# Attention backward: reciprocals of the softmax row sums moved from VectorE to GpSimd, and the row factors spread over four iterations

## The chip, the cores and the metric

One NeuronCore of a Trainium2 chip runs one program. The metric is the device time of the program in microseconds; the figure before the change is the median of three runs, 2174.07 us (2173.19 to 2174.79). A profile is one further execution, taken with the hardware profiler. The engines are named as in the profile: PE (TensorE's matmuls), PEld (its weight loads), DVE (VectorE), ACT (ScalarE), POOL (GpSimd) and SP (SyncE, which here only issues DMAs).

## The reference

What is computed is the output and all gradients of

```python
xn = layernorm(x)
s = attention(xn, wqkv, wo)           # 32 heads of 16, 2048 rows, softmax(q k^T / 4) v
g = silu(mlp(xn, w1, b1, w2, b2))     # layernorm, 512 -> 1792 (gelu) -> 512
out = x + s * g
```

with x of 2048 x 512 in bf16, for a given gradient of `out`. The change touches the attention alone. Per row of queries it needs L (the sum of the exponentials, the softmax' denominator), 1/L, and delta = (row sum of p times dp) in the form of a sum that is divided by L. With them O, dQ, dK and dV are formed.

## The kernel before

The program has three stages: projections, MLP forward and all preparations (to about 220 us), the attention forward and backward in one pass (to about 1845 us), and the remaining gradients.

**The attention's loop.** `attention_core` goes over 64 blocks: 16 pairs of heads (`p`) times 4 chunks of 512 queries (`qc`). A block has 16 iterations, one per 128 keys, so the loop variable `g` runs over 1024 iterations and 20 more, and g % 16 is the iteration within a block. The order of all instructions is written out by hand in the loop body (L1395 to L1445); each engine executes its own instructions in that order. In iteration g:

- `emit_d(g)` and `emit_s(g + 1)` (PE): dp^T of this iteration, in two halves into three rotating PSUM buffers (`d`), and the scores of the next one into a single PSUM buffer (`s`).
- `emit_exp(g + 1)` (ACT, L1155): the exponentials `ets`.
- `emit_z(g - 20)` (PE, L1365): the sums `Z` for dK and dV of a block that began 20 iterations earlier. Their weights are W2 (first four of eight iterations, one query chunk of 128 in each: iterations 4 to 7 and 12 to 15 of a block) and W1 (the other four: iterations 8 to 11, and 0 to 3). Iteration 4 thus reads the part of W2 for the first query chunk of the block before, iteration 6 the one for the third.
- `emit_x(g - 1)` (PE, L1263, L1266, L1270): the sums `X` for O, L, delta and dQ; the last group reads `gts`, DVE's product of the iteration before.
- `emit_T(g - 1)` (PE, L1223, L1227): transposes of the exponentials into one PSUM buffer `tT`, which `emit_cT` (ACT, L1239) and `emit_cO` (DVE, L1246) copy to `ek`.
- `emit_mult(g)`: POOL copies a part of `ets` to `gts` (L1184), DVE forms the two products `gts` = d times ets (L1186). Between the two products stand, where due, the copy of X (L1279, in iteration 0) and `emit_acc` (DVE, L1377, L1379): the sum of Z over the query chunks, in iterations 3 and 11. After the last query chunk of a pair of heads `emit_acc` also lets POOL cast the sum (`ob`, L1383) and issue two DMAs that store it (L1386). For one half of the sums that falls into iteration 11 of a pair's first block, for the other into iteration 3 of its second block.
- `emit_dmat(g)` (SP): a DMA transpose of every second `gts` to `gk`, which Z reads later. `gts` has four buffers, each for two iterations.
- Loads of the next pair's operands are issued from POOL's queue in chosen iterations (6, 9, 12, 15), each behind a tiny copy (`tick`, L1435) that waits for DVE's product of that iteration.

**The end of a block.** When a block's X is complete, DVE copies it (`xs`), PE transposes it in two halves (`emit_XT`, iterations 1 and 6 of the next block), and at the start of the iteration after (2 and 7) DVE copies the transposed half back (`emit_xt`, L1305) and `emit_fin` runs. For the half that holds L (iteration 2): DVE's reciprocal rL (L1325), then POOL's chain: W2 = q times rL (L1326), ndl = delta sum times rL (L1328), ndr = ndl times rL (L1330), and the two halves of W1 (L1331, L1332). For the other half (iteration 7): O, and dQ over four instructions (L1337 to L1344). W2 has one buffer, W1 two. For the last block both halves run in the iterations right after the loop's last block, with no attention beside them.

Of the kernel before, what the change touches and what calls it, by code (L numbers as in the profile page):

```python
# [9 lines left out]
f32 = mybir.dt.float32  # L10
ACT = mybir.ActivationFunctionType
ALU = mybir.AluOpType
# [1069 lines left out]
def attention_core(ctx, ctx_r, tc, k, grads, Oall, dQall, dKVT_out, ident_f32, ident_bf, npairs=16, nqc=4):  # L1082
    nc = tc.nc
# [13 lines left out]
    finp = sb("finp", 1)  # L1097
# [13 lines left out]
    W2 = wp.tile([128, 4, 2, 32], bf16, name="W2")  # L1111
    nc.gpsimd.memset(W2[:, :, :, 0:16], 0.0)
    for i in range(2):
        W1 = wp.tile([128, 4, 2, 32], bf16, name=f"W1_{i}")
# [6 lines left out]
    blk = [dict(Gk={}, Ek={}) for _ in range(NB)]  # L1121
    cur = {}

    def a_unit(g):
        return (g // 16, g % 16) if 0 <= g < NSTEP else None
# [178 lines left out]
        j, h = f  # L1304
        nc.vector.tensor_copy(out=blk[j]["xs"][:, 256 * h:256 * h + 256], in_=blk[j].pop("XT"))  # L1305

    def emit_fin(g):
        f = fin_half(g)
        if f is None:
            return  # L1310
        j, half = f
        p, qc = blocks[j]
        NQq = k.op0["NATQq"]
        NQd = k.op0["NATQd"]
        xf = blk[j]["xs"][:]
        XE = xf[:, 0:256].rearrange("q (b h c) -> q b h c", b=4, h=2)
        XG = xf[:, 256:512].rearrange("q (b h c) -> q b h c", b=4, h=2)
        W1, W2 = WT[j % 2]
        st0 = qc * 4
        nqs = NQq[:, st0:st0 + 4, :, :]  # L1320
        ndo = NQd[:, st0:st0 + 4, :, :]
        bc = lambda ap: ap.to_broadcast([128, 4, 2, 16])
        if half == 1:
            rL = finp.tile([128, 4, 2, 1], f32, name="rL")
            nc.vector.reciprocal(out=rL[:], in_=XG[:, :, :, 17:18])  # L1325
            nc.gpsimd.tensor_tensor(out=W2[:, :, :, 16:32], in0=nqs, in1=bc(rL[:]), op=ALU.mult)  # L1326
            ndl = finp.tile([128, 4, 2, 1], f32, name="ndl")
            nc.gpsimd.tensor_tensor(out=ndl[:], in0=XG[:, :, :, 0:1], in1=rL[:], op=ALU.mult)  # L1328
            ndr = finp.tile([128, 4, 2, 1], f32, name="ndr")
            nc.gpsimd.tensor_tensor(out=ndr[:], in0=ndl[:], in1=rL[:], op=ALU.mult)  # L1330
            nc.gpsimd.tensor_tensor(out=W1[:, :, :, 0:16], in0=ndo, in1=bc(rL[:]), op=ALU.mult)  # L1331
            nc.gpsimd.tensor_tensor(out=W1[:, :, :, 16:32], in0=nqs, in1=bc(ndr[:]), op=ALU.mult)  # L1332
            blk[j]["r"] = rL, ndl
            return
        rL, ndl = blk[j].pop("r")
        Ov = Oall[:, st0:st0 + 4, p * 32:(p + 1) * 32].rearrange("q b (h c) -> q b h c", h=2)
        nc.gpsimd.tensor_tensor(out=Ov, in0=XE[:, :, :, 16:32], in1=bc(rL[:]), op=ALU.mult)  # L1337
        t1 = finp.tile([128, 4, 2, 16], f32, name="t1")
        nc.gpsimd.tensor_tensor(out=t1[:], in0=XE[:, :, :, 0:16], in1=bc(ndl[:]), op=ALU.mult)
        nc.gpsimd.tensor_tensor(out=t1[:], in0=XG[:, :, :, 1:17], in1=t1[:], op=ALU.add)  # L1340
        rL4 = finp.tile([128, 4, 2, 1], f32, name="rL4")
        nc.gpsimd.tensor_scalar(out=rL4[:], in0=rL[:], scalar1=0.25, scalar2=None, op0=ALU.mult)
        dQv = dQall[:, st0:st0 + 4, p * 32:(p + 1) * 32].rearrange("q b (h c) -> q b h c", h=2)
        nc.gpsimd.tensor_tensor(out=dQv, in0=t1[:], in1=bc(rL4[:]), op=ALU.mult)  # L1344
        blk[j].pop("xs")
# [49 lines left out]
    for g in range(NSTEP - ZOFF):  # L1395
        cur["g"] = g
        a = a_unit(g)
        if a is not None:
            j, kb = a
            p, qc = blocks[j]  # L1400
            if kb == 0 and qc == 0:
                L = natq_loads(k, k.op0, p, nc.gpsimd.dma_start) if p > 0 else []
                if p + 1 < npairs:
                    L += op_load_list(k, OP[(p + 1) % 2], p + 1, nc.gpsimd.dma_start)
                else:
                    L += grads.tail_loads(nc.gpsimd.dma_start)
                for i, f in enumerate(L):
                    late.append((g + 16 * (i // 4) + 6 + 3 * (i % 4), f))
        emit_cO(g - 2)
        if a_unit(g - 2) is not None:  # L1410
            emit_xt(g - 1)
            emit_fin(g - 1)
        emit_d(g, 0)
        emit_s(g + 1, 0)
        emit_s(g + 1, 1)
        emit_d(g, 1)
        emit_exp(g + 1)
        emit_z(g + ZOFF)
        emit_x(g - 1, "e")
        emit_x(g - 1, "l")  # L1420
        if g % 16 == 2:
            emit_x(g - 2, "g")
        if g % 16 != 1:
            emit_x(g - 1, "g")
        st_T.pop(g - 2, None)
        emit_T(g - 1)
        emit_XT(g)
        emit_mult(g)
        if a_unit(g - 1) is None:
            emit_xt(g)  # L1430
            emit_fin(g)
        for it in [x for x in late if x[0] <= g]:
            late.remove(it)

            nc.gpsimd.tensor_copy(out=tick[:], in_=st_gt[g][0:1, kb % 2, 7, 126:128])  # L1435
            it[1]()
        if g >= NSTEP:
            grads.tail_mid(g - NSTEP)
        emit_cT(g - 1)
        emit_dmat(g)  # L1440
        st_gt.pop(g - 3, None)
        st_et.pop(g - 12, None)
        if g == NSTEP:
            ctx_r.close()
            grads.tail_open(ps_t, ps_s, ps_d)  # L1445


def full_kernel(ctx, tc, A_x, A_wqkv, A_wo, B_x, B_w1, B_b1, B_w2, B_b2, grad_out,
                out_0, out_1, out_2, out_3, out_4, out_5, out_6, out_7, dbg=None):
    nc = tc.nc  # L1450
    dbg = dbg or {}
    k = K()
    persist = ctx.enter_context(tc.tile_pool(name="persist", bufs=1))
    k.ident_bf = persist.tile([128, 128], bf16, name="ident_bf")
    make_identity(nc, k.ident_bf[:])
    k.ident_f = persist.tile([128, 128], f32, name="ident_f")
    make_identity(nc, k.ident_f[:])
    k.eps_t = persist.tile([128, 1], f32, name="eps_t")
    nc.vector.memset(k.eps_t[:], EPS)
    k.rstd1 = persist.tile([128, NT], f32, name="rstd1")  # L1460
    k.rstd2 = persist.tile([128, NT], f32, name="rstd2")
    persist.tile([128, 224], mybir.dt.uint8, name="pad_to_256")

    def scratch(name, shape, dt=bf16):
        if name in dbg:
            return dbg[name]
        return tc.dram_tile(list(shape), dt, name=name)
    k.XN_s = scratch("XN_s", [S, D])
    k.Y_s = scratch("Y_s", [S, D])
    k.DSO_s = scratch("DSO_s", [S, D])  # L1470
    k.H1T_s = scratch("H1T_s", [F, S])
    k.HGT_s = scratch("HGT_s", [F, S])
    k.WKV_s = scratch("WKV_s", [D, 1024])
    k.DH1_s = scratch("DH1_s", [4, 4, 128, 4, 4, 128])
    k.NAT_s = scratch("NAT_s", [NPAIR, 128, NT, 2 * NATW])
    k.NATQq_s = scratch("NATQq_s", [NPAIR, 128, NT, 32])
    for n in ("KT_s", "VT_s", "QT_s", "DOT_s"):
        setattr(k, n, scratch(n, [D, S]))
    k.UT_s = scratch("UT_s", [H, S])
    k.NATQd_s = scratch("NATQd_s", [NPAIR, 128, NT, 32])  # L1480
    k.GB_s = scratch("GB_s", [S, 2, D])
    k.dKVT_s = scratch("dKVT_s", [H * 32, S])

    with ExitStack() as cO, tc.manual_schedule():
        op0p = cO.enter_context(tc.tile_pool(name="op0", bufs=1, side="right", reuse_waits="tile"))
        k.op0 = make_op(nc, op0p, 0)
        k.Lc = op0p.tile([128, 32], bf16, name="Lc")
        nc.gpsimd.memset(k.Lc[:], 0.0)
        nc.gpsimd.memset(k.Lc[:, 17:18], 1.0)
        op0p.tile([128, 96], mybir.dt.uint8, name="pad_to_256r")  # L1490
        kv, nat, q, do, natd = op_loads(k, k.op0, 0, nc.sync.dma_start)
        first = dict(kv=kv, q=lambda: (nat(), q()), do=lambda g: (do(g * 512, g * 512 + 512), natd(g * 4, g * 4 + 4)))
        with ExitStack() as cP:
            Pre(cP, tc, k, first, A_x, A_wqkv, A_wo, B_w1, B_b1, B_w2, B_b2, grad_out)
        pO = cO.enter_context(tc.tile_pool(name="persistO", bufs=1, reuse_waits="tile"))
        k.Oall = pO.tile([128, NT, D], bf16, name="Oall", tag="Oall")
        k.dQall = pO.tile([128, NT, D], bf16, name="dQall", tag="dQall")
        grads = Grads(cO, tc, k, pO, op0p, A_x, grad_out, A_wqkv, A_wo, B_w1, B_w2,
                      (out_0, out_1, out_2, out_3, out_4, out_5, out_6, out_7))
        with ExitStack() as cB:  # L1500
            attention_core(cB, cB.enter_context(ExitStack()), tc, k, grads, k.Oall, k.dQall, k.dKVT_s, k.ident_f, k.ident_bf)
        grads.run()
# [56 lines left out]
```

## Time and profile before

| what | value |
|---|---|
| median of three runs | 2174.07 us |
| the profiled execution | 2176.54 us, of which the span of the trace is 2174.8 us |
| attention, first to last exponential's start | 210 to 1832 us of the span |
| PE, DVE, ACT, POOL busy in 640 to 840 us | 200.0, 187.0, 184.5, 83.8 us of 200 |
| DVE reciprocal (L1325) | 64 x 203 ns |
| POOL's chain for W2 and W1 (L1326 to L1332) | 398, 197, 204, 402, 401 ns each |

The first part of the profile's page gives busy time per engine, the groups of instructions give line, engine, operation, the tiles written and read, the count, the busy time in us with the mean in ns, and the idle time of the engine before them with what ended it. The timeline gives start, duration, line, operation and count of neighbouring instructions of one kind. The waits list who waited for whom: total us, number of times, the longest. Matmuls overlap in PE, and one that waits in PE's queue counts as busy.

### The profile page before, as it was taken

What the parts mean: (1) busy time and instruction counts of PE and PEld (TensorE: products, weight loads), DVE (VectorE), ACT (ScalarE), POOL (GpSimd) and SP (SyncE); (2) the same over time, 40 slices, a digit from 0 to 9 for tenths busy, and PEclk for the clock granted to TensorE, in tenths of its full rate; (3) what the DMA queues carried; (4) which work ended last, traced back from release to release, by engine and by line L of the source; (5) the groups of instructions that cost most, each with busy time, mean ns of one, the idle gap of its engine ahead of it and who ended that gap; (6) DMA issues with size and microseconds to landing.
All of it is one profiled execution on the core that took longest, in us unless ns stands there. A gap on an engine that the chain in (4) does not pass through costs nothing.

```text
span 2174.8 us, 74927 instructions
## 1 busy us (share of the span) xinstructions
PE 2135.9 (98%) x30663; PEld 1169.9 (54%) x30663; DVE 1900.2 (87%) x3524; ACT 1781.4 (82%) x2482; POOL 868.4 (40%) x2396
## 2 busy tenths in 40 slices
PE   7998999999999999999999999999999999999999
PEld 4444555555555555555555555555555555444444
DVE  7677899999999999999999999999999998897637
ACT  5754999999999999999999999999999997784214
POOL 4286334343444434343444344444434344510003
PEclk9999999999999999999999999999999999999999
DMA  7986999999999999999999999999999999999875
GB/s 243 275 275 211 187 203 199 203 205 201 202 206 199 204 201 200 206 199 194 206 201 204 201 207 201 198 207 200 200 207 204 197 213 222 283 267 233 235 207 176
DMA packets 1416601, 461.17 MB, mean 212 GB/s; under 512 B 1329150, under 2 KB 1400446, under 8 KB 1416256
## 3 DMA queue, kind: packets, MB, share of 16 engines
q1 hardware_dynamic: 1401952, 425.44, 101.3%
q0 software_dynamic: 12720, 29.37, 4.8%
q8 instruction: 240, 3.93, 0.8%
q10 hardware_dynamic: 1584, 1.57, 0.2%
q14 instruction: 105, 0.86, 0.1%
HBM read 62.79 MB, written 64.75 MB: 59 GB/s over the span
## 4 chain that ended last, share of the span: by engine, by line
PE 93%; DMA 3%; DVE 3%; ACT 1%; POOL 1%; issue 1%; SPq 0%; DVEq 0%; POOLq 0%; ACTq 0%
PE tT L1223 22%; PE d L1168 15%; PE Z L1365 15%; PE X L1270 6%; PE X L1263 5%; PE X L1266 5%; PE s L1146 3%; PE ps_dy L940 2%; PE ps_h L374 2%; PE ps_m L389 2%; PE ps_dw L1014 2%; PE ps_dw L773 2%; PE ps_dh L906 2%; PE ps_dwkv L858 1%; PE tT L1297 1%; PE ps_dxa L1058 1%
## 5 line engine op out<-in xcount | busy, mean ns | idle before, releaser
L1186 DVE TENSOR_TENSOR gts<-d,ets 128x512 bf16<-128x512 f32 x2048 | 1302.5, 683 | 20.0 <-PE d L1168 4.4
L1155 ACT ACTIVATE ets<-s 128x1024 bf16<-128x1024 f32 x1024 | 1051.3, 1027 | 16.2 <-PE d L1168 3.6
L1239 ACT COPY ek<-tT 128x448 f32<-128x448 f32 (+1 forms) x1024 | 524.7, 512 | 118.0 <-PE tT L1223 29.6
L1223 PE MATMUL tT<-ident_bf,ets 128*128 128x128 bf16 x6790 | 557.9, 221 | 0.0
L1223 PEld LDWEIGHTS <-ets 128*128 128x128 bf16 x6790 | 382.4, 98 | 211.0 <-issue 196.7
L1168 PE MATMUL d<-QDT,KVT 32*128 32x512 bf16 x2048 | 470.3, 384 | 2.7 <-DVE gts L1186 2.6
L1184 POOL COPY gts<-ets 128x128 bf16<-128x128 bf16 x1024 | 280.2, 295 | 391.2 <-ACT ets L1155 383.6
L1146 PE MATMUL s<-QDT,KVT 32*128 32x512 bf16 x2048 | 400.9, 379 | 3.0 <-ACT ets L1155 2.4
L1365 PE MATMUL Z<-gk,W 128*32 128x512 bf16 x2304 | 302.9, 389 | 1.3 <-DVE acc L1379 1.1
L1263 PE MATMUL X<-ets,NAT 128*32 128x256 bf16 x4096 | 290.4, 273 | 0.0
L1266 PE MATMUL X<-ets,Lc 128*32 128x256 bf16 x4096 | 290.2, 273 | 0.0
L1270 PE MATMUL X<-gts,NAT 128*17 128x256 bf16 x4096 | 289.8, 273 | 0.0
L1365 PEld LDWEIGHTS <-W 128*32 128x32 bf16 x4096 | 105.5, 93 | 240.0 <-issue 226.2
L1168 PEld LDWEIGHTS <-KVT 32*128 32x128 bf16 x2048 | 148.3, 90 | 114.4 <-issue 21.5
L1365 PE MATMUL Z<-ek,W 128*32 128x512 bf16 x1792 | 203.7, 389 | 0.0
L1266 PEld LDWEIGHTS <-Lc 128*32 128x32 bf16 x4096 | 110.2, 97 | 108.5
L1246 DVE COPY ek<-tT 128x64 f32<-128x64 f32 x378 | 85.0, 225 | 88.1 <-ACT ek L1239 72.5
L1435 POOL COPY tick<-gts 1x2 bf16<-1x2 bf16 x205 | 35.7, 174 | 313.9 <-DVE gts L1186 313.9
L1146 PEld LDWEIGHTS <-KVT 32*128 32x128 bf16 x2048 | 142.6, 90 | 13.4 <-issue 7.2
L1270 PEld LDWEIGHTS <-NAT 128*17 128x17 bf16 x4096 | 114.0, 91 | 14.5 <-issue 1.7
L1263 PEld LDWEIGHTS <-NAT 128*32 128x32 bf16 x4096 | 108.8, 96 | 7.2 <-issue 7.2
L1326 POOL TENSOR_TENSOR W<-NATQq,rL 128x128 bf16<-128x128 bf16 x64 | 25.4, 398 | 148.0 <-DVE rL L1325 115.7
(256 smaller groups left out, 2476.2 us busy)
## 6 DMA issues: line engine op xcount, KB each, us to landing
gk<-gts SPq DMA_TRANSPOSE x512, 5.4
H1T_s<-h1r SPq DMA_DIRECT2D x28, 256.0 KB, 3.2
HGT_s<-hgT SPq DMA_DIRECT2D x8, 896.0 KB, 4.6
DH_s<-stg SPq DMA_DIRECT2D x12, 512.0 KB, 3.6
hch<-DH_s SPq DMA_DIRECT2D x12, 512.0 KB, 4.8
gp<-H1T_s SPq DMA_DIRECT2D x9, 512.0 KB, 5.4
out_dram<-ob_w POOLq DMA_DIRECT2D x36, 128.0 KB, 4.1
NAT_s<-NS SPq DMA_DIRECT2D x4, 1056.0 KB, 5.9
```

The source lines that it names most:

```text
L1146: nc.tensor.matmul(s[:, hj, :], lhsT=op["KVT"][r:r + 32, kb * 128:(kb + 1) * 128], rhs=op["QDT"][r:r + 32, qc * 512:(qc + 1) * 512], start ...
L1155: nc.scalar.activation(out=st_et[g].rearrange("k b h q -> k h b q"), in_=cur["s"][:].rearrange("k h (b q) -> k h b q", b=4), func=ACT.Exp)
L1168: nc.tensor.matmul(d[:], lhsT=op["KVT"][r:r + 32, kb * 128:(kb + 1) * 128], rhs=op["QDT"][r:r + 32, qc * 512:(qc + 1) * 512], start=True, ...
L1184: nc.gpsimd.tensor_copy(out=gts[:, kb % 2, 8, :], in_=st_et[g][:, b // 2, b % 2, :])
L1186: nc.vector.tensor_tensor(out=gts[:, kb % 2, 4 * hj:4 * hj + 4, :], in0=st_d.pop((g, hj))[:].rearrange("k (b q) -> k b q", b=4), in1=st_et ...
L1223: nc.tensor.transpose(tb[:, i - cut(g), :], et[:, b // 2, b % 2, :], ident_bf[:])
L1239: nc.scalar.copy(out=blk[j]["Ek"][kb // 4][:, kb % 4, c:7].rearrange("q i k -> q (i k)").bitcast(f32), in_=st_T[g][:, 0:(7 - c) * 64])
L1246: nc.vector.tensor_copy(out=blk[g // 16]["Ek"][kk // 4][:, kk % 4, i].bitcast(f32), in_=st_T[g][:, 448:512])
L1263: nc.tensor.matmul(X[r:r + 32, 0:256], lhsT=NATt[:, kb, hj, 1:33], rhs=ev, start=(kb == 0), stop=False, skip_group_check=True, tile_positi ...
L1266: nc.tensor.matmul(X[r:r + 32, 256:512], lhsT=Lc[:], rhs=ev, start=False, stop=False, skip_group_check=True, tile_position=(0, r))
L1270: nc.tensor.matmul(X[r:r + 17, 256:512], lhsT=NATt[:, kb, hj, 0:17], rhs=gv, start=False, stop=(kb == 15), skip_group_check=True, tile_pos ...
L1365: nc.tensor.matmul(Z[r:r + 32, :], lhsT=WT[j % 2][1 - part][:, qb, hj, :], rhs=mv, start=(part == 0 and qb == 0), stop=(part == 1 and qb = ...
```

## The change

The reciprocal leaves DVE. POOL forms it as L to the power -1 and one Newton step, r (2 - L r), for the first two query chunks of 128 with the first half of W2 in iteration 2, and for the other two in iteration 3. The rest of the chain follows in iteration 4 (ndl, ndr, first half of W1) and iteration 5 (second half of W1). Of the second half, O is formed in iteration 7 and dQ in iteration 8. All these pieces now stand after `emit_mult` of their iteration and no longer at its start. For the last block the four pieces run one after the other in one iteration. A constant tile of -1 (32 bytes per partition) is added and the padding is cut by as much.

```diff
-    def emit_fin(g):
+    def emit_fin(g, ph):
         f = fin_half(g)
-        if f is None:
+        if f is None or (f[1] == 0 and ph > 1):
             return
...
         if half == 1:
-            rL = finp.tile([128, 4, 2, 1], f32, name="rL")
-            nc.vector.reciprocal(out=rL[:], in_=XG[:, :, :, 17:18])
-            nc.gpsimd.tensor_tensor(out=W2[:, :, :, 16:32], in0=nqs, in1=bc(rL[:]), op=ALU.mult)
-            ndl = finp.tile([128, 4, 2, 1], f32, name="ndl")
-            nc.gpsimd.tensor_tensor(out=ndl[:], in0=XG[:, :, :, 0:1], in1=rL[:], op=ALU.mult)
-            ndr = finp.tile([128, 4, 2, 1], f32, name="ndr")
-            nc.gpsimd.tensor_tensor(out=ndr[:], in0=ndl[:], in1=rL[:], op=ALU.mult)
-            nc.gpsimd.tensor_tensor(out=W1[:, :, :, 0:16], in0=ndo, in1=bc(rL[:]), op=ALU.mult)
-            nc.gpsimd.tensor_tensor(out=W1[:, :, :, 16:32], in0=nqs, in1=bc(ndr[:]), op=ALU.mult)
-            blk[j]["r"] = rL, ndl
-            return
-        rL, ndl = blk[j].pop("r")
+            if ph == 0:
+                blk[j]["r"] = tuple(finp.tile([128, 4, 2, 1], f32, name=n) for n in ("rL", "ndl", "ndr"))
+            rL, ndl, ndr = blk[j]["r"]
+            if ph < 2:
+                b2 = slice(2 * ph, 2 * ph + 2)
+                L, r, n = XG[:, b2, :, 17:18], rL[:, b2], ndl[:, b2]
+                nc.gpsimd.tensor_tensor(out=r, in0=L, in1=k.minus[:, b2], op=ALU.pow)
+                nc.gpsimd.tensor_tensor(out=n, in0=L, in1=r, op=ALU.mult)
+                nc.gpsimd.tensor_scalar(out=n, in0=n, scalar1=-1.0, scalar2=2.0, op0=ALU.mult, op1=ALU.add)
+                nc.gpsimd.tensor_tensor(out=r, in0=r, in1=n, op=ALU.mult)
+                nc.gpsimd.tensor_tensor(out=W2[:, b2, :, 16:32], in0=nqs[:, b2], in1=r.to_broadcast([128, 2, 2, 16]), op=ALU.mult)
+            elif ph == 2:
+                nc.gpsimd.tensor_tensor(out=ndl[:], in0=XG[:, :, :, 0:1], in1=rL[:], op=ALU.mult)
+                nc.gpsimd.tensor_tensor(out=ndr[:], in0=ndl[:], in1=rL[:], op=ALU.mult)
+                nc.gpsimd.tensor_tensor(out=W1[:, :, :, 0:16], in0=ndo, in1=bc(rL[:]), op=ALU.mult)
+            elif ph == 3:
+                nc.gpsimd.tensor_tensor(out=W1[:, :, :, 16:32], in0=nqs, in1=bc(ndr[:]), op=ALU.mult)
+            return
+        rL, ndl, ndr = blk[j]["r"]
...
-        nc.gpsimd.tensor_tensor(out=Ov, in0=XE[:, :, :, 16:32], in1=bc(rL[:]), op=ALU.mult)
+        if ph == 0:
+            nc.gpsimd.tensor_tensor(out=Ov, in0=XE[:, :, :, 16:32], in1=bc(rL[:]), op=ALU.mult)
+            return
...
         if a_unit(g - 2) is not None:
             emit_xt(g - 1)
-            emit_fin(g - 1)
...
         emit_mult(g)
+        for ph in range(4):
+            if a_unit(g - 2 - ph) is not None:
+                emit_fin(g - 1 - ph, ph)
         if a_unit(g - 1) is None:
             emit_xt(g)
-            emit_fin(g)
+            for ph in range(4):
+                emit_fin(g, ph)
...
+    k.minus = persist.tile([128, 4, 2, 1], f32, name="minus")
+    nc.gpsimd.memset(k.minus[:], -1.0)
```

More of the change, by code (lines that the diff above doesn't have):

```diff
@@ L1461, in full_kernel @@
     k.rstd2 = persist.tile([128, NT], f32, name="rstd2")
-    persist.tile([128, 224], mybir.dt.uint8, name="pad_to_256")
+    k.minus = persist.tile([128, 4, 2, 1], f32, name="minus")
+    nc.gpsimd.memset(k.minus[:], -1.0)
+    persist.tile([128, 192], mybir.dt.uint8, name="pad_to_256")
     def scratch(name, shape, dt=bf16):
```

## The prediction

> **What bounds the kernel now.** I read the page first, then the waits of PE, then one block of the attention in the timeline.
>
> ```profile
> span 2174.8 us, 74927 instructions
> ...
> PE 2135.9 (98%) x30663; PEld 1169.9 (54%) x30663; DVE 1900.2 (87%) x3524; ACT 1781.4 (82%) x2482; POOL 868.4 (40%) x2396
> ...
> L1186 DVE TENSOR_TENSOR gts<-d,ets 128x512 bf16<-128x512 f32 x2048 | 1302.5, 683 | 20.0 <-PE d L1168 4.4
> L1155 ACT ACTIVATE ets<-s 128x1024 bf16<-128x1024 f32 x1024 | 1051.3, 1027 | 16.2 <-PE d L1168 3.6
> ```
>
> PE looks full, and the waits of PE between 300 and 1800 us name a single one:
>
> ```profile
> PE d L1168 <- DVE gts L1186: 1.0, 1, 1.0
> ```
>
> That is no proof that PE waits for nobody: a matmul that waits inside PE's queue counts as busy. So I read the starts in the timeline. Below, engine by engine (start, duration, line, operation, count), are iterations 2 to 6 of one of the 64 blocks; "iteration" counts its 16 steps from 0. Iteration 2 starts at about 748.1, iteration 3 at 749.77.
>
> ```profile
> 748.58 0.42 DVE L1305 COPY xs<-tT 128x256 f32<-128x256 f32 x1
> 749.03 0.20 DVE L1325 RECIPROCAL rL<-xs 128x8 f32<-128x8 f32 x1
> 749.15 1.88 DVE L1186 TENSOR_TENSOR gts<-d,ets 128x512 bf16<-128x512 f32 x3
> 750.95 0.68 DVE L1379 TENSOR_TENSOR acc<-Z,acc 128x512 f32<-128x512 f32 x1
> 751.54 1.28 DVE L1186 TENSOR_TENSOR gts<-d,ets 128x512 bf16<-128x512 f32 x2
> ```
>
> ```profile
> 749.77 0.39 PE L1168 MATMUL d<-QDT,KVT 32*128 32x512 bf16 x1
> 749.77 0.39 PE L1146 MATMUL s<-QDT,KVT 32*128 32x512 bf16 x2
> 749.89 0.37 PE L1168 MATMUL d<-QDT,KVT 32*128 32x512 bf16 x1
> ...
> 751.38 0.39 PE L1146 MATMUL s<-QDT,KVT 32*128 32x512 bf16 x2
> ...
> 751.71 0.40 PE L1365 MATMUL Z<-gk,W 128*32 128x512 bf16 x4
> ...
> 752.15 0.41 PE L1270 MATMUL X<-gts,NAT 128*17 128x256 bf16 x4
> 752.50 0.56 PE L1223 MATMUL tT<-ident_bf,ets 128*128 128x128 bf16 x7
> ...
> 754.93 0.40 PE L1365 MATMUL Z<-gk,W 128*32 128x512 bf16 x4
> ```
>
> ```profile
> 750.30 1.03 ACT L1155 ACTIVATE ets<-s 128x1024 bf16<-128x1024 f32 x1
> ...
> 751.88 1.03 ACT L1155 ACTIVATE ets<-s 128x1024 bf16<-128x1024 f32 x1
> ...
> 753.52 1.03 ACT L1155 ACTIVATE ets<-s 128x1024 bf16<-128x1024 f32 x1
> ```
>
> ```profile
> 749.38 0.40 POOL L1326 TENSOR_TENSOR W<-NATQq,rL 128x128 bf16<-128x128 bf16 x1 [2.19 <-PE d L1168]
> 749.74 0.20 POOL L1328 TENSOR_TENSOR ndl<-xs,rL 128x8 f32<-128x8 f32 x1
> 750.01 0.20 POOL L1330 TENSOR_TENSOR ndr<-ndl,rL 128x8 f32<-128x8 f32 x1
> ...
> 751.69 0.61 POOL L1383 CAST ob<-acc 128x512 bf16<-128x512 f32 x1 [0.29 <-DVE acc L1379]
> 752.60 1.14 POOL L1386 DMA_DIRECT2D dKVT_s<-ob  x2 [0.30 <-POOL ob L1383]
> 753.74 0.53 POOL L1184 COPY gts<-ets 128x128 bf16<-128x128 bf16 x2
> ```
>
> Two loops run at nearly one speed. An exponential (1.03) ends at 751.33 and the next s starts at 751.38, because s has one PSUM buffer; 0.50 later the next exponential starts. That closes at about 1.58 us (750.30 to 751.88). PE's own list of matmuls takes about as long, so where PE is late the step lengthens: 751.88 to 753.52 is 1.64.
>
> DVE makes PE late in that last step. From 748.58 on DVE runs without a gap: copy, reciprocal, three products, the sum into acc, and then the second product of iteration 3, from 751.54 to 752.22. The X matmuls of iteration 4 need it: four of them, from 752.15, and the transposes follow only at 752.50, which is 0.28 after the product's end. So this step is paced by DVE, and the reciprocal is part of the run that is late.
>
> **What the change removes.** DVE's reciprocal: 0.20 us per block, 13 us in all. Not all of it can be used. The first product of iteration 3 needs its d, which PE issues at 749.77, and a product cannot start before d has run (0.39) and been handed over: about 750.26 (0.1 after d, as elsewhere in the block) against 750.35 now (749.15 plus two of 0.60, as three take 1.88). So the late product comes only some 0.09 earlier, and the transposes with it. The worth of a DVE that is in time can be read from the trace. In one block an exponential is held up just ahead of this place (the mark in its row, second fence) and DVE catches up; the seven steps that follow stand beside those of the block before:
>
> ```profile
> 548.13 1.03 ACT L1155 ACTIVATE ets<-s 128x1024 bf16<-128x1024 f32 x1
> ...
> 559.20 1.03 ACT L1155 ACTIVATE ets<-s 128x1024 bf16<-128x1024 f32 x1
> ```
>
> ```profile
> 573.61 1.02 ACT L1155 ACTIVATE ets<-s 128x1024 bf16<-128x1024 f32 x1 [0.16 <-DVE gts L1186]
> ...
> 584.60 1.03 ACT L1155 ACTIVATE ets<-s 128x1024 bf16<-128x1024 f32 x1
> ```
>
> 11.07 against 10.99: 0.08 us per block, not 0.2, since PE's list and the exponentials take over as limits. I take **0.08 per block** (bounds: 0, and 0.2 if all of it counts).
>
> **What it adds, all on POOL.** For each half of a block: a power, a product, a product-and-sum, a product, and half of the write to W2. POOL's groups by shape give the prices:
>
> ```profile
> L1331 POOL TENSOR_TENSOR W<-NATQd,rL 128x128 bf16<-128x128 bf16 x64 | 25.7, 402 | 0.0
> ...
> L1342 POOL TENSOR_SCALAR rL<-rL 128x8 f32<-128x8 f32 x64 | 14.6, 228 | 0.0
> L1330 POOL TENSOR_TENSOR ndr<-ndl,rL 128x8 f32<-128x8 f32 x64 | 13.1, 204 | 5.0
> L1328 POOL TENSOR_TENSOR ndl<-xs,rL 128x8 f32<-128x8 f32 x64 | 12.6, 197 | 0.0
> ```
>
> A small instruction is 0.20, a scalar one 0.23, half of a W write lies between 0.20 and 0.40, so 0.30. One that waits for the instruction ahead of it starts 0.07 after its end (749.94 to 750.01); I use 0.08. With P for the power, a half takes P + 0.08 + 0.28 + 0.31 + 0.28 + 0.30 = **P + 1.25**. No row shows a power on POOL. Below, it is a plain product: 0.20. Above, a routine as long as twelve small instructions: 2.4. I take **P = 0.6**, an estimate of three plain passes (a logarithm, a product, an exponential); it is nearer to the small rows than to the other end.
>
> The Trainium skill speaks against the move: its page "GPSIMD Engine Reference" (4.1 Engine selection) sends elementwise work to VectorE, with GpSimd about 2x slower on two inputs. The rows agree only for the number of instructions: 0.20 for eight elements on POOL, 0.20 for DVE's reciprocal of eight. The sum by that rule would have a power of 0.4 and come out 3.4 us below mine.
>
> **Where it lies.** The first half starts 0.15 after the copy of xs ends (as 749.23 to 749.38 now), at 749.15, and W2's first half is ready at 750.40 + P. Z first reads it in iteration 4, at 751.71 now: 1.25 to spare, so nothing for P up to 1.25. The second half follows in iteration 3 behind one copy of gts (0.30), ready at about 752.0 + 2P, and is read in iteration 6, at 754.93: nothing either, in 49 of 64 blocks.
>
> In the 15 blocks like the one shown it isn't hidden. There POOL writes out the dK/dV sum in iteration 3: the order on POOL puts the cast of ob and its two DMA issues ahead of the second half. They end at 753.74 now, 753.65 with acc 0.09 earlier; the copy that starts at 753.74 shows that POOL was held until then. The second half is ready at 753.65 + P + 1.25 = 754.90 + P, Z can start 0.06 later (the step from the product's end at 749.83 to d at 749.89), and it starts at 754.93 now. PE loses 0.03 + P: 0.63 with P = 0.6, and hardly any of it comes back, since PE's list is nearly as long as a step.
>
> The last block has nothing beside it, and there all four pieces run in one go.
>
> ```profile
> 1837.87 0.42 DVE L1305 COPY xs<-XT 128x256 f32<-128x256 f32 x1 [1.50 <-PE XT L1297]
> ...
> 1838.68 0.40 POOL L1326 TENSOR_TENSOR W<-NATQq,rL 128x128 bf16<-128x128 bf16 x1 [5.15 <-DVE rL L1325]
> ...
> 1842.31 1.02 PE L1365 MATMUL Z<-ek,W 128*32 128x512 bf16 x12
> ```
>
> From 1838.44 two halves take 2P + 2.5, the two small factors and both halves of W1 1.28: W1 is there at 1842.2 + 2P, and Z with ek, now at about 1842.3, waits 2P - 0.1 = 1.1.
>
> Cost nothing: the memset and the pad; the copies of gts, which come ahead of the pieces now (SP's transpose also waits for DVE's product at 752.22); the row factors and W1, read first in iteration 8; O and dQ, read only after the attention; the ticks and loads behind them, which wait for DVE's products anyway. If gts' four buffers did not cover late copies, DVE would wait for the transposes.
>
> **Sum.** 49 x 0.08 = 3.9 gained, 15 x 0.63 = 9.5 and 1.1 lost: +6.7 us. In general -3.5 + 17P for P up to 1.25. The profiled execution took 2176.54 (span 2174.8 and 1.7 around it) and would take 2183.2; the median shown, 2174.07, becomes **2180.8**.
>
> **Rivals.**
> 1. The power is cheap (P up to 0.35): gain and loss cancel. P = 0.2 gives 2174.0. For: eight elements cost no more than the fixed part of an instruction. Against: a power is no single product.
> 2. Faster: the second half is in time in the 15 blocks too. It must be ready by 754.87, so it must start by 753.0 with P = 0.6; that happens if POOL's DMA issues do not hold what is behind them, so that it starts at 752.6. Then 64 x 0.08 = 5.1 is gained and, with P = 0.3, 0.5 lost at the end: 2169.5. Against: the copy at 753.74.
> 3. The power is a long routine. From P = 1.25 every block waits in iteration 4 too, for P - 1.25; P = 1.5 adds 16 to the 22 of the formula: 2212; P = 2.4 gives about 2285.
> 4. POOL's extra instructions slow DVE's products.
>
> ```profile
> L1186 DVE TENSOR_TENSOR gts<-d,ets x2048: 678/682/694, 214.3 to 1834.6; 128x512 bf16<-128x512 f32 x187
> ```
>
> The products spread by 16 ns at most, with POOL busy 40% of the time, so eight of them per block cost up to 0.13 us, more than the gain: +6.7 + 64 x 0.13 = 2189.1. The Trainium skill's page "GPSIMD Engine Reference" (8. Key points) has the two engines share their SBUF interfaces, with contention where DVE reads two SBUF inputs; here one of the two is PSUM, and the trace shows none.
>
> **Chances.** Forecast (P from 0.35 to 1.25) 0.46, rival 1 0.24, rival 2 0.13, rival 3 0.13, rival 4 0.04. Range: from rival 2 (2169) to P = 1.3, where the waits in iteration 4 begin (-3.5 + 22.1 + 3.2: 2196); left out are rival 3 and little else. The forecast's own range is 2176 to 2192. 0.2% is 4.3 us, about what a measurement of this kernel can tell from no change: faster 0.13 (rival 2), same 0.32 (rival 1, and 0.08 of the forecast with P below 0.47), slower 0.55.
>
> **What would show it.** In the changed profile: the power's mean (0.6); the step of iteration 4 shorter by some 0.08; in 15 blocks Z of iteration 6 late by 0.6 behind W, with PE's weight load waiting for POOL's W; DVE's busy time 13 us lower. I am wrong if Z of iteration 6 does not wait in those blocks, if the power is over 1.25, or if DVE's late product is as late as before.

## The result and the profile after

| | before | after |
|---|---|---|
| median of six runs each | 2173.63 us (2171.23 to 2174.91) | 2190.80 us (2188.00 to 2194.18) |
| profiled execution | 2176.54 us, span 2174.8 | 2191.19 us, span 2189.5 |

The ratio is 1.0082, with a 95% interval of 1.0072 to 1.0092: the change costs 15.6 to 20.0 us. It is slower, as forecast, by 17.2 us where 6.7 were forecast.

First the page of the kernel after: span, busy times, and the three groups that matter (line, engine, operation, tiles, count, then busy us and mean ns, then idle time ahead and what ended it).

```profile
span 2189.5 us, 75517 instructions
...
PE 2128.8 (97%) x30614; PEld 1171.5 (54%) x30663; DVE 1895.5 (87%) x3460; ACT 1784.7 (82%) x2482; POOL 1084.5 (50%) x2973
...
L1186 DVE TENSOR_TENSOR gts<-d,ets 128x512 bf16<-128x512 f32 x2048 | 1307.6, 682 | 24.6 <-PE d L1168 5.7
L1155 ACT ACTIVATE ets<-s 128x1024 bf16<-128x1024 f32 x1024 | 1051.5, 1027 | 16.7 <-PE d L1168 4.0
L1374 PE MATMUL Z<-gk,W 128*32 128x512 bf16 x2304 | 303.3, 389 | 19.6 <-POOL W L1334 18.3
```

Z has become one of the groups with idle time ahead of it, nearly all ended by POOL's W. The waits of PE in the kernel after between 300 and 1800 us (total us, times, longest) say how often:

```profile
PE Z L1374 <- POOL W L1334: 17.5, 16, 1.2
PE Z L1374 <- DVE acc L1386: 0.2, 1, 0.2
```

Sixteen waits, 17.5 us. Fifteen of them, 1.11 to 1.20 us each, are Z of iteration 6 in the 15 blocks that write out a dK/dV sum while their row factors are made. The sixteenth, 0.56 us, is Z of iteration 4 in a single block of query chunk 2: there POOL stood idle for 3.22 us ahead of a load's DMA issue, and the first half of W2 came too late (done at 988.01, Z at 988.06). POOL's timeline of that block in the kernel after:

```profile
984.55 0.49 POOL L61 DMA_DIRECT2D QDT<-UT_s  x1 [3.22 <-issue]
...
985.75 1.04 POOL L1330 TENSOR_TENSOR rL<-xs,minus 128x4 f32<-128x4 f32 x1
...
987.72 0.29 POOL L1334 TENSOR_TENSOR W<-NATQq,rL 128x64 bf16<-128x64 bf16 x1
```

In the kernel before the same issue is 3.21 us late, and no Z waits for it; what holds it stays open. One of the 15 blocks is the block that the prediction showed; it now stands 4.38 us later (Z of iteration 4 at 756.09 instead of 751.71). Its POOL timeline in the kernel after (start, duration, line, operation, count, idle time before):

```profile
753.47 1.04 POOL L1330 TENSOR_TENSOR rL<-xs,minus 128x4 f32<-128x4 f32 x1 [0.60 <-DVE xs L1305]
...
755.43 0.29 POOL L1334 TENSOR_TENSOR W<-NATQq,rL 128x64 bf16<-128x64 bf16 x1
755.67 0.29 POOL L1184 COPY gts<-ets 128x128 bf16<-128x128 bf16 x1
756.00 0.61 POOL L1392 CAST ob<-acc 128x512 bf16<-128x512 f32 x1
756.91 1.20 POOL L1395 DMA_DIRECT2D dKVT_s<-ob  x2 [0.30 <-POOL ob L1392]
758.12 1.04 POOL L1330 TENSOR_TENSOR rL<-xs,minus 128x4 f32<-128x4 f32 x1
759.24 0.20 POOL L1331 TENSOR_TENSOR ndl<-xs,rL 128x4 f32<-128x4 f32 x1
759.54 0.19 POOL L1332 TENSOR_SCALAR ndl<-ndl 128x4 f32<-128x4 f32 x1
759.81 0.20 POOL L1333 TENSOR_TENSOR rL<-rL,ndl 128x4 f32<-128x4 f32 x1
760.08 0.29 POOL L1334 TENSOR_TENSOR W<-NATQq,rL 128x64 bf16<-128x64 bf16 x1
```

The first half is done at 755.72, 0.37 us ahead of its reader at 756.09. The second starts only at 758.12, when the second DMA issue has ended (756.91 + 1.20 = 758.11), and is done at 760.37. PE's Z and ACT's exponentials of the same block in the kernel after:

```profile
756.09 0.40 PE L1374 MATMUL Z<-gk,W 128*32 128x512 bf16 x4
...
757.64 0.40 PE L1374 MATMUL Z<-gk,W 128*32 128x512 bf16 x4
...
760.43 0.40 PE L1374 MATMUL Z<-gk,W 128*32 128x512 bf16 x4 [1.12 <-POOL W L1334]
```

```profile
756.25 1.02 ACT L1155 ACTIVATE ets<-s 128x1024 bf16<-128x1024 f32 x1
...
757.83 1.03 ACT L1155 ACTIVATE ets<-s 128x1024 bf16<-128x1024 f32 x1
...
759.39 1.03 ACT L1155 ACTIVATE ets<-s 128x1024 bf16<-128x1024 f32 x1
...
762.16 1.02 ACT L1155 ACTIVATE ets<-s 128x1024 bf16<-128x1024 f32 x1
```

Z of iteration 6 starts 0.06 after W's end and 1.12 late. The exponentials show both sides of the change in one block: the step of iteration 4 is 1.58 instead of 1.64 (756.25 to 757.83), the step of the wait is 2.77 instead of some 1.56.

Comparing the start of a block's first exponential with that of the next block in both traces gives a ledger by kind of block (median change per block; the block above is of the second kind):

| blocks | kernel after, change of a block's length |
|---|---|
| query chunk 0 (16) | -0.075 us |
| query chunk 1, store in the way (15) | +1.117 us |
| query chunk 2 (16) | -0.064 us in eight, +0.010 in the other eight |
| query chunk 3 (16, the last without a next block) | -0.059 us |

15 x 1.117 = 16.8 us lost, 16 x 0.075 + 8 x 0.064 - 8 x 0.010 + 16 x 0.059 = 2.6 us gained. To this comes the end of the attention in the kernel after, where PE waits for POOL with nothing beside it:

```profile
1855.31 0.62 PE L1374 MATMUL Z<-gk,W 128*32 128x512 bf16 x8 [0.29 <-DVE acc L1388]
1856.73 0.61 PE L1374 MATMUL Z<-gk,W 128*32 128x512 bf16 x8 [0.81 <-POOL W L1334]
1857.90 0.39 PE L1374 MATMUL Z<-ek,W 128*32 128x512 bf16 x1 [0.55 <-POOL W L1340]
```

From the last exponential's start to the last Z's start it takes 15.27 us (1846.03 to 1861.30) where it took 13.54 (1832.15 to 1845.69): 1.7 us. The sum is 16.8 - 2.6 + 1.7 = 15.9 us, or 16.5 with the one block of the sixteenth wait, which is 0.58 longer; both lie inside the measured 15.6 to 20.0. The two profiled executions differ by 14.7; before lost 1.38 us in one block to a rare stall that after did not have, and the stage behind the attention varies: from the last exponential to the end it took 342.7 us in before, 343.5 in after, and 339.5 to 345 in the experiments.

### The profile page after: what moved, and what is told of

The parts are those of the page before. It is cut to its first block, busy times and chain, and to the rows that moved or that the text cites. A ratio compares the mean times of both kernels' runs of the same rounds, so it can differ in the third digit from the quotient of the medians.

```text
span 2189.5 us, 75517 instructions
## 1 busy us (share of the span) xinstructions
PE 2128.8 (97%) x30614; PEld 1171.5 (54%) x30663; DVE 1895.5 (87%) x3460; ACT 1784.7 (82%) x2482; POOL 1084.5 (50%) x2973
## 4 chain that ended last, share of the span: by engine, by line
PE 84%; DVE 5%; POOL 5%; DMA 2%; issue 2%; ACT 1%; POOLq 0%; DVEq 0%; SPq 0%; ACTq 0%
PE tT L1223 20%; PE Z L1374 14%; PE d L1168 13%; PE X L1270 5%; PE X L1263 5%; PE X L1266 5%; PE s L1146 3%; DVE gts L1186 2%; PE ps_dy L940 2%; PE ps_dw L1014 2%; PE ps_m L389 2%; PE ps_h L374 2%; PE ps_dw L773 2%; PE ps_dh L906 2%; POOL rL L1330 2%
## 5 line engine op out<-in xcount | busy, mean ns | idle before, releaser
L1186 DVE TENSOR_TENSOR gts<-d,ets 128x512 bf16<-128x512 f32 x2048 | 1307.6, 682 | 24.6 <-PE d L1168 5.7
L1239 ACT COPY ek<-tT 128x448 f32<-128x448 f32 (+1 forms) x1024 | 524.7, 512 | 127.8 <-PE tT L1297 20.1
L1184 POOL COPY gts<-ets 128x128 bf16<-128x128 bf16 x1024 | 292.1, 294 | 329.5 <-ACT ets L1155 323.2
L1270 PE MATMUL X<-gts,NAT 128*17 128x256 bf16 x4096 | 284.9, 273 | 0.0
L1168 PEld LDWEIGHTS <-KVT 32*128 32x128 bf16 x2048 | 151.6, 90 | 114.4 <-issue 21.6
L1146 PEld LDWEIGHTS <-KVT 32*128 32x128 bf16 x2048 | 146.1, 90 | 17.0 <-issue 8.5
L1330 POOL TENSOR_TENSOR rL<-xs,minus 128x4 f32<-128x4 f32 x128 | 131.5, 1028 | 40.8 <-DVE xs L1305 40.6
L1270 PEld LDWEIGHTS <-NAT 128*17 128x17 bf16 x4096 | 113.6, 91 | 10.5 <-issue 0.7
```

What stands on the lines that cost most here:

```text
L1146: nc.tensor.matmul(s[:, hj, :], lhsT=op["KVT"][r:r + 32, kb * 128:(kb + 1) * 128], rhs=op["QDT"][r:r + 32, qc * 512:(qc + 1) * 512], start ...
L1168: nc.tensor.matmul(d[:], lhsT=op["KVT"][r:r + 32, kb * 128:(kb + 1) * 128], rhs=op["QDT"][r:r + 32, qc * 512:(qc + 1) * 512], start=True, ...
L1184: nc.gpsimd.tensor_copy(out=gts[:, kb % 2, 8, :], in_=st_et[g][:, b // 2, b % 2, :])
L1186: nc.vector.tensor_tensor(out=gts[:, kb % 2, 4 * hj:4 * hj + 4, :], in0=st_d.pop((g, hj))[:].rearrange("k (b q) -> k b q", b=4), in1=st_et ...
L1239: nc.scalar.copy(out=blk[j]["Ek"][kb // 4][:, kb % 4, c:7].rearrange("q i k -> q (i k)").bitcast(f32), in_=st_T[g][:, 0:(7 - c) * 64])
L1270: nc.tensor.matmul(X[r:r + 17, 256:512], lhsT=NATt[:, kb, hj, 0:17], rhs=gv, start=False, stop=(kb == 15), skip_group_check=True, tile_pos ...
```

## The experiments

My theory (A): Z waits in the 15 blocks only because the store stands ahead of the second half on POOL, and the wait is 0.03 us plus the power's time. The rivals: (B) POOL's extra load costs something in every block wherever the store stands; (C) spreading the factors over four iterations is what costs; (D) the relief of DVE is worth its full 0.2 us per block and (E) it is worth nothing. The first four kernels ran on one chip (before: 2174.29 us), the last two on another (before: 2172.28).

### The store behind the second half

```diff
-            nc.gpsimd.tensor_copy(out=ob[:], in_=av)
-            dv = dKVT_out[p * 64:(p + 1) * 64, :].rearrange("r (a b s) -> r a b s", a=2, b=2)
-            for b in range(2):
-                nc.gpsimd.dma_start(out=dv[:, kp, b, :], in_=ob[b * 64:(b + 1) * 64, :])
+            def store():
+                ...
+            cur["store"] = store
...
         for ph in range(4):
             if a_unit(g - 2 - ph) is not None:
                 emit_fin(g - 1 - ph, ph)
+        if "store" in cur:
+            cur.pop("store")()
```

> The changed kernel, with POOL's cast of the dK/dV sum and its two DMA issues put behind the second half of the reciprocal instead of ahead of it. Theory A (the loss is the wait of Z in iteration 6 of 15 blocks, because the store of 2.05 us stands ahead of the second half on POOL): the second half is ready about 2 us earlier, Z does not wait, and the 15 x 1.12 us go: 2172 to 2175 us, the blocks with a store as short as the others. Rival B (POOL's longer work as such costs, by slowing DVE or by late copies of gts, wherever the store stands): the time stays above 2185.

Measured: 2172.35 us, ratio 0.9991 (0.9982 to 1.0). The POOL timeline of the same block in this kernel:

```profile
750.64 0.29 POOL L1334 TENSOR_TENSOR W<-NATQq,rL 128x64 bf16<-128x64 bf16 x1
750.88 0.29 POOL L1184 COPY gts<-ets 128x128 bf16<-128x128 bf16 x1
751.13 1.01 POOL L1330 TENSOR_TENSOR rL<-xs,minus 128x4 f32<-128x4 f32 x1
...
753.05 0.29 POOL L1334 TENSOR_TENSOR W<-NATQq,rL 128x64 bf16<-128x64 bf16 x1
753.29 0.61 POOL L1394 CAST ob<-acc 128x512 bf16<-128x512 f32 x1
754.20 1.19 POOL L1397 DMA_DIRECT2D dKVT_s<-ob  x2 [0.29 <-POOL ob L1394]
```

and its PE's Z of iterations 4, 5 and 6:

```profile
751.31 0.40 PE L1374 MATMUL Z<-gk,W 128*32 128x512 bf16 x4
...
752.86 0.40 PE L1374 MATMUL Z<-gk,W 128*32 128x512 bf16 x4
...
754.45 0.40 PE L1374 MATMUL Z<-gk,W 128*32 128x512 bf16 x4
```

The second half is ready at 753.34, 1.1 us ahead of its reader, and Z goes on at an even pace. PE's waits in this kernel between 300 and 1800 us:

```profile
PE Z L1374 <- POOL W L1334: 0.6, 1, 0.6
```

From 17.5 us to 0.6, with all of POOL's new instructions still there. The wait that is left is the one behind the late load. The blocks with a store are now 0.061 us shorter than in before, like the others (0.060 to 0.072), and as short as with no reciprocal at all (0.060 to 0.074 in the fourth experiment). That holds A up, and B falls: but for the one block with the late load, the order of three instructions on one queue was the whole loss inside the attention. What the parts give, 3.5 gained and 1.7 lost at the end, is 1.8; measured is 1.9, with an interval from 0 to 3.9.

### The reciprocal back on DVE, the four pieces kept

```diff
         if a_unit(g - 2) is not None:
             emit_xt(g - 1)
+            emit_rec(g - 1)
...
-                nc.gpsimd.tensor_tensor(out=r, in0=L, in1=k.minus[:, b2], op=ALU.pow)
...
+                r = rL[:, b2]
```

> The changed kernel, but with the reciprocal on DVE as before; only the splitting of W2's write and the spreading of the chain over four iterations are left of the change. Theory A: without the power and the Newton step the second half takes 0.3 us behind the store and is in time; nothing is gained on DVE either, so within 3 us of before, 2171 to 2177. Rival C (the spreading itself is what costs, by making W1, O or the copies late): above 2182.

Measured: 2175.84 us, ratio 1.001 (1.0001 to 1.0019). Blocks are 0.005 to 0.009 us longer than in before, and PE waits for no W between 300 and 1800 us. Splitting the write to W2 and spreading the factors costs some 0.5 us by the blocks, inside the measured 0.2 to 4.1: C falls.

### A product in place of the power

This kernel leaves the reciprocal out; the instructions around it stay.

```diff
-                nc.gpsimd.tensor_tensor(out=r, in0=L, in1=k.minus[:, b2], op=ALU.pow)
+                nc.gpsimd.tensor_tensor(out=r, in0=L, in1=k.minus[:, b2], op=ALU.mult)
...
-    nc.gpsimd.memset(k.minus[:], -1.0)
+    nc.gpsimd.memset(k.minus[:], 2.0 ** -11)
```

> The changed kernel with a plain product (L times a constant) in the place of the power; the power is left out, everything else stays, the store ahead of the second half too. Theory A with the prediction's formula, -3.5 + 17 P for a power of P, at P = 0.2: about 2174 (2172 to 2177), Z late by some 0.25 us in the 15 blocks. Rival C (the number and the order of the pieces cost, not the power's 1.04 us): above 2182.

Measured: 2175.27 us, ratio 1.0003 (0.9994 to 1.0012). The group by shape, and the waits of PE between 300 and 1800 us, both of this kernel:

```profile
L1330 POOL TENSOR_TENSOR rL<-xs,minus 128x4 f32<-128x4 f32 x128 | 25.4, 199 | 40.6 <-DVE xs L1305 40.4
```

```profile
PE Z L1374 <- POOL W L1334: 4.0, 15, 0.3
```

The instruction that stands in for the power takes 0.20 us, and fifteen waits of 0.27 us remain; the blocks with a store are 0.251 us longer than in before. The theory asks for 0.03 + 0.20. So the loss goes with the power's duration, as the formula has it, and at this price the change would have been neutral. The late load is there too (3.21 us), and with so short a first half no Z waits for it.

### No reciprocal at all

```diff
-            rL = finp.tile([128, 4, 2, 1], f32, name="rL")
-            nc.vector.reciprocal(out=rL[:], in_=XG[:, :, :, 17:18])
+            rL = k.minus
```

(on the kernel before, with `k.minus` set once to a constant).

> The kernel before without the reciprocal: a constant stands in its place, nothing else is changed. It measures alone what DVE's 0.20 us per block are worth. Theory A (the first product of iteration 3 must wait for its d, so only 0.09 us come through, and 0.06 to 0.08 of a block's time): 2168.5 to 2171. Rival D (all 0.2 us of DVE count): about 2160. Rival E (DVE is off the path): 2173 to 2174.5.

Measured: 2169.74 us, ratio 0.9982 (0.9973 to 0.999): 2.2 to 5.9 us less than before. Blocks are 0.074, 0.063 and 0.060 us shorter for query chunks 0, 1 and 3; of those of chunk 2 eight are 0.060 shorter and eight 0.010 longer, the same split as in the kernel after. That is 3.5 us in all. DVE's 13 us of reciprocals are worth no more, even if their work vanishes: D falls, and so does E.

### The store behind the half, and the last block's reciprocals on DVE

The first experiment's kernel with one more edit:

```diff
+                if j == NB - 1:
+                    nc.vector.reciprocal(out=r, in_=L)
+                else:
+                    nc.gpsimd.tensor_tensor(out=r, in0=L, in1=k.minus[:, b2], op=ALU.pow)
...
```

> The store behind the second half, and in the last block, which has nothing beside it, the reciprocals by DVE again. Theory A: the wait of 1.8 us at the end of the attention goes (Z with ek waits for W1 there, 2P - 0.1 in the prediction), on top of the first experiment: 2169.5 to 2172, below both kernels. Rival: the end is covered by the stage behind it (its DMAs end as late as before): the same as the first experiment, 2172 to 2173.

Measured: 2171.61 us, ratio 0.9991 (0.9982 to 1.0). The trace shows what the edit did: from the last exponential's start to the last Z's it takes 13.5 us (1828.2 to 1841.7) again, where the first experiment took 15.2 (1828.3 to 1843.5). The third experiment, with a product for the power, took 13.6. The 1.7 us at the end of the attention are thus the power's. The total does not show them: against the kernel before the ratio is the same as the first experiment's. Whether the stage behind the attention takes them back, or they are lost in runs that differ by some us, stays open. This is the best form of the change that I found, by the blocks some 3.6 us better than before and by the total at most 0.2%.

### One piece instead of two halves

```diff
-            if ph < 2:
-                b2 = slice(2 * ph, 2 * ph + 2)
+            if ph == 0:
+                b2 = slice(0, 4)
...
```

> The changed kernel with the whole reciprocal and the whole of W2 in one piece in iteration 2, so eight elements in one power and nothing left behind the store. If the power's time goes with its elements (0.2 fixed and 0.84 for four), eight take 1.9 us, W2 is ready at 749.15 + 1.9 + 1.35 = 752.4 on the clock of the block shown in the prediction, Z of iteration 4 reads it at 751.7 and waits 0.7 to 0.8 in every block: 64 x 0.75 = 48, 2215 to 2225 us. If the power is a fixed cost (eight take about 1.1), W2 is ready at 751.6, in time: 2171 to 2175, better than the halves.

Measured: 2194.31 us, ratio 1.0097 (1.0084 to 1.0111). Both expectations missed: the power of eight elements took neither twice the time of four nor the same. Power by shape in this kernel, and POOL in one block without a store:

```profile
L1330 POOL TENSOR_TENSOR rL<-xs,minus 128x8 f32<-128x8 f32 x64 | 107.2, 1675 | 40.9 <-DVE xs L1305 40.9
```

```profile
499.42 1.68 POOL L1330 TENSOR_TENSOR rL<-xs,minus 128x8 f32<-128x8 f32 x1 [0.60 <-DVE xs L1305]
...
502.03 0.40 POOL L1334 TENSOR_TENSOR W<-NATQq,rL 128x128 bf16<-128x128 bf16 x1
```

The whole W2 takes 3.01 us (499.42 to 502.43), more than the 2.56 between the earliest start of the factors and Z of iteration 4 in the prediction's block (749.15 to 751.71). PE in this block:

```profile
502.49 0.40 PE L1374 MATMUL Z<-gk,W 128*32 128x512 bf16 x4 [0.37 <-DVE gts L1186]
```

and its waits between 300 and 1800 us:

```profile
PE Z L1374 <- DVE gts L1186: 16.8, 45, 0.4
PE Z L1374 <- POOL W L1334: 3.7, 7, 1.3
```

These 52 waits are all Z of iteration 4, one in each block of this stretch but six. By their medians blocks are 0.31 to 0.33 us longer than in before, except for the eight of query chunk 2 that gain nothing in the ledger: seven of these are some 0.13 longer, and one, the block with the late load, is 1.32 longer. That is about 56 x 0.32 + 7 x 0.13 + 1.3 = 20.1 of the 22.0 us. This is the prediction's third rival, reached by a longer piece instead of a longer power. The row of the wait must be read with care: it names DVE's product, but Z starts 0.06 after W's end at 502.43, the same 0.06 as in the kernel after, where the row names W. In all 52 waits Z starts 0.05 to 0.06 after W's end, while the last product ended anywhere from 0.00 to 1.19 ahead of it. So the 45 waits that are put down to DVE are POOL's as well.

## Why the prediction was right in sign and short in size

The mechanism was right, and one price was not. The measured 2190.80 lies near the upper end of the forecast's own range, 2176 to 2192, which its wide bounds for the power had left open; the point, 2180.8, was 10 us too low. By its steps:

1. **The gain.** Right in kind: DVE is no longer late. The last d of iteration 3, which waits for a buffer that DVE reads, started a median of 0.11 us after the scores beside it in before and starts 0.01 after them now; the transposes of iteration 4 come 0.08 earlier against their step; the step of iteration 4 is 1.58 instead of 1.64, and not 0.2 but 0.059 to 0.075 us per block come back. In the prediction's block of the kernel after the transposes start 1.03 us behind the scores (1.12 in before, 751.38 to 752.50):

```profile
755.77 0.39 PE L1146 MATMUL s<-QDT,KVT 32*128 32x512 bf16 x2
...
756.80 0.56 PE L1223 MATMUL tT<-ident_bf,ets 128*128 128x128 bf16 x7
```

   Taken was 0.08 for 49 blocks, 3.9 us; measured 2.6. Eight blocks gain nothing: in them another short pause had already let DVE catch up, as in the very block from which the 0.08 was read.
2. **The power.** This is the step that failed. The estimate was 0.6, three plain passes; it is 1.04. Rows of the kernel after, POOL's groups by shape:

```profile
L1330 POOL TENSOR_TENSOR rL<-xs,minus 128x4 f32<-128x4 f32 x128 | 131.5, 1028 | 40.8 <-DVE xs L1305 40.6
L1334 POOL TENSOR_TENSOR W<-NATQq,rL 128x64 bf16<-128x64 bf16 x128 | 37.4, 292 | 10.1 <-POOL rL L1333 0.2
L1333 POOL TENSOR_TENSOR rL<-rL,ndl 128x4 f32<-128x4 f32 x128 | 25.6, 200 | 10.7
L1331 POOL TENSOR_TENSOR ndl<-xs,rL 128x4 f32<-128x4 f32 x128 | 25.3, 197 | 10.0
L1332 POOL TENSOR_SCALAR ndl<-ndl 128x4 f32<-128x4 f32 x128 | 24.4, 191 | 11.7
```

   The other instructions cost what was taken for them: a half takes 2.25 us in the timeline (758.12 to 760.37), P + 1.25 gives 2.29. With P = 1.04 the formula, -3.5 + 17P, gives +14.2 instead of +6.7. The 7.5 us between them are most of the 10.5 that were missing; the smaller gain adds 1.3, the wait's own excess (1.117 for 1.07, 15 times) 0.7 and the block with the late load 0.6.
3. **The wait in the 15 blocks.** Right. 0.03 + 1.04 = 1.07 was asked for, 1.12 is in the row, and hardly any of it comes back, as said: the block is 1.117 longer than in before, and 1.18 longer than in the first experiment, where it keeps its gain of 0.061. The third experiment confirms the formula at a second price, the first shows that it is the order on POOL alone.
4. **The first half and the other blocks.** Right but for one block: P stayed under 1.25, and in the ledger no other kind of block is over 0.01 us longer by its median. In the block of the sixteenth wait the first half started late because POOL was held by a load's issue; the loads had been put at nothing, and here one costs 0.56 us once the power is 1.04.
5. **The end.** 2P - 0.1 gives 2.0; measured 1.7.
6. **Edits at nothing.** Right apart from that load: the second experiment has all of them, without the power and the Newton step, and comes to within 0.005 to 0.009 us per block.

The rivals: a cheap power would have given 2175, as the third experiment shows, but the power isn't cheap. Rival 2 asked that DMA issues let later work pass; the power starts 0.01 after they end. Rival 3 is real but begins above this power's time. Rival 4 is wrong (its eight products per block were a choice, a block has 32, but nothing hangs on the count); DVE's products in the kernel after (min, median and max ns):

```profile
L1186 DVE TENSOR_TENSOR gts<-d,ets x2048: 676/680/693, 214.7 to 1848.5; 128x512 bf16<-128x512 f32 x187
```

They were 678/682/694, so with POOL busy for 50% of the span instead of 40% they are no slower. The Trainium skill's page "GPSIMD Engine Reference" (8. Key points) names contention on the shared SBUF interfaces for DVE instructions in a 2-port mode or with two SBUF inputs; the products have one of their two inputs in PSUM, and the trace shows none. By the Trainium skill's rule on engines (same page, 4.1 Engine selection, about a factor of two on two inputs) 0.4 was the estimate for the power; the run gives 1.04, and 0.20 for a product of eight elements, as long as DVE's reciprocal of eight.

One announced sign was wrong in itself: DVE's busy time fell by 4.7 us (1900.2 to 1895.5), not 13. Busy time counts overlapping records once. The 64 reciprocals overlap their neighbours (749.03 + 0.20 reaches past 749.15) and make up only 7.9 us of the busy time of before, and the records of DVE's products overlap less now: their group counts 1307.6 us instead of 1302.5, though the mean of one fell from 683 to 682 ns.

## What to carry to other kernels

Work that is moved to an engine with time to spare must be placed against that engine's queue in every variant of the iteration: here 15 of 64 blocks, in which a store stood ahead of the piece with the deadline, decided the sign, and moving the store behind it took the loss away. Measure or bound from both sides an operation that no row shows before anything else is refined; most of the miss was in one such term. And what a relieved engine gives back is only the part by which it was later than the next limit, here 0.06 to 0.075 of 0.2 us.

## What the runs showed of the hardware

- A power on POOL takes 1.03 us on average for 128x4 elements in f32 and 1.68 for 128x8. An estimate from these two sizes alone is 0.38 us fixed and 0.16 for each element of a partition. A product takes 0.20 for either.
- Two DMA issues on POOL hold what is behind them for their whole 1.20 us; the next instruction started 0.01 later.
- A load's DMA issue on POOL can start late and hold what is behind it: in one block, the same in all eight profiled kernels, it came after 3.21 to 3.22 us of idle time for which the profile names no cause.
- The profile can put a wait for several semaphores down to the wrong engine block after block (45 of 52 waits in the last experiment); the gap of 0.06 us behind W's end, the same in all of them, tells who it was.
